# Pooled attention, SoLU and SiLU on one core: other places in the step table of the first SiLU matmul, and one reload issued by ACT

## The chip, the core and the metric

The kernel runs on one core of one Trainium2 chip. A core has five engines that work side by side, each through its own instructions in order: PE (matmuls, into PSUM), DVE, ACT and POOL (element by element work), and SP, which here only starts DMA transfers. DMA transfers started from any queue run on the core's 16 DMA engines. The metric is the device time of one execution in microseconds (us). Before the change it is 1367.52 us, the median of three runs (1366.87 to 1371.12).

## The reference

Three blocks follow each other, all in float32, on 8 x 576 = 4608 tokens:

```
k_p, v_p = k, v averaged over groups of 8 positions
attn = softmax(q @ k_p.T / 8) @ v_p                  # 8 heads of 64 -> x: 4608 x 512
h = x @ w_in (512 x 1024); solu = h * softmax(h)
x = layer_norm(solu) * g_ln @ w_out (1024 x 512)
h = x @ w_in2 (512 x 2048); g = h / (1 + exp(-h))    # SiLU
out = g @ w_out2 (2048 x 512)
```

The change lies in `h = x @ w_in2` and its SiLU, "the first SiLU matmul" below.

## The kernel before

Every operand is kept as a pair of rounded parts, high and low, and a product is three matmuls (high*high, high*low, low*high). The high part is made by ACT (a copy that rounds), the low part by DVE (a subtraction, line 529). Both SiLU matmuls use seven products of sums of quarters instead of eight products of quarters, so sums and differences of the quarters of both operands have to be made too.

The first SiLU matmul runs from about 609 to 1000 us of the profiled span. It is 12 passes, n = 0 to 11. A pass takes 768 tokens (one of six groups) and half of the 2048 columns of the weights; passes 0 to 5 use the first half, that is the weight sets 0 and 1, passes 6 to 11 the second half, sets 2 and 3. A pass has four steps (i = 0 to 3) of seven products, 28 products in all, of six matmuls each (line 709). Each product fills one of eight PSUM banks, which are taken in turn, and has one reader: the first and the third of a step are copied to SBUF by ACT (lines 724 and 729), the others are read by DVE additions (line 719). POOL adds two more sums per step into the result tile `gt`. ACT then takes SiLU of `gt` in two halves (line 677), and SP writes `gt` to DRAM as `gd` (line 679). There are two `gt` tiles, so step i must find the write of step i - 2 landed.

Beside the products other work is laid on the engines by a table of places. `plan(n, work, first)` puts each piece `(at, f)` at place `first + at * (28 - first) // 28` of pass n; place p is issued behind the reader of product p. On ACT, DVE, POOL and SP the order of the instructions is exactly the order in which the program writes them, so these numbers set the order of each engine's queue, and an instruction that has to wait holds up all that stands behind it on its engine. The pieces that matter here:

- `load_tokens(n)` (line 625, on SP): 768 tokens of the next pass, `x2r`, 1536 KB. There is one such buffer, so the load waits until the tokens before have been read for the last time.
- `tokens(n)` (lines 627 to 658): sums of token quarters on POOL (from pass 1 on), high parts on ACT (line 640), low parts on DVE, for the next pass. The first high part, of `r11`, and the first sum are its first pieces.
- `load_quad(q)` (line 540, on SP): the raw quarters of a weight set, `w2r`, two transfers.
- `quad_sums(q)` (lines 585 to 605), in passes 1 and 2: the sums S1 to S4 of weight sets 2 and 3, split (ACT line 592, DVE line 529) and written to DRAM as `wsd` (line 596), since the buffers for sets 2 and 3 are still in use. `load_sums(q)` (line 611) brings them back, four transfers of 512 KB: set 2 in pass 5 behind place 15, set 3 in pass 6 behind place 0. `quad_rest` makes the other three of each set at that time, from `w2r`.
- `load_rows(f)` (line 748, on SP): raw rows of the last weights, `wr`, in two buffers which `quad_sums` uses for its results before; `w2o_block(f)` (lines 752 to 784), from pass 3 on, splits them and writes them to DRAM as `wod` (line 775).

Each DMA gets one of eight landing semaphores, and a DMA that gets a semaphore again first waits for the one before on it to land.

Of the kernel before, what the change touches and what calls it, by code (L numbers as in the profile page):

```python
# [9 lines left out]
F32 = mybir.dt.float32  # L10
# [34 lines left out]
L11, L12, S4, L22, S1, S2, S3 = range(7)  # L45
# [37 lines left out]
def pooled_attention__solu__silu_kernel(  # L83
# [13 lines left out]
    nc = tc.nc  # L97
# [437 lines left out]
    wq, w2r = {}, {}  # L535

    def load_quad(q):
        w2r[q] = [pools["wr"].tile([P, 2, 512], F32, tag=f"w2r{h}", name="w2r") for h in range(2)]
        for h in range(2):
            nc.sync.dma_start(w2r[q][h], w2if[q][:, 2 * h : 2 * h + 2])  # L540
# [44 lines left out]
    def quad_sums(q):  # L585

        sum_, _, _, src = quarter(q)
        out = {}

        def hi(k, j):  # L590
            out[k] = pools["wx"].tile([P, 2, 512], F32R, tag=f"a{k % 2}", name="wo")
            nc.scalar.activation(out[k][:, 0], src[j], AF.Copy)

        def lo(k, j):
            sub(nc.vector, out[k][:, 1], src[j], out[k][:, 0].bitcast(F32))
            nc.sync.dma_start(wsd[q][k], out[k].bitcast(F32))

        work = [(2, lambda: sum_(S1)), (4, lambda: sum_(S2)), (12, lambda: sum_(S3))]
        for k, j in enumerate((S2, S1, S3)):
            work += [(7 + 4 * k, lambda k=k, j=j: hi(k, j)), (9 + 4 * k, lambda k=k, j=j: lo(k, j))]  # L600

        def fourth():
            sub(nc.vector, src[L12], src[L12], src[S2])

        return work + [(16, fourth), (19, lambda: hi(3, L12)), (21, lambda: lo(3, L12))]

    def load_sums(q):
        pool = pools["wq1" if q % 2 else "wq0"]
        for k, j in enumerate((S2, S1, S3, S4)):
            wq[q, j] = pool.tile([P, 2, 512], F32R, tag=f"w{j}", name=f"w2s{j}")  # L610
            nc.sync.dma_start(wq[q, j].bitcast(F32), wsd[q][k])

    def quad_rest(q, at):

# [8 lines left out]
    def load_tokens(n):  # L623
        x2r[n] = pools["x2r"].tile([P, KC, G2], F32, tag="x2r", name="x2r")
        nc.sync.dma_start(x2r[n], x2d[n % NG2])
# [58 lines left out]
    def plan(n, work, first=0, last=28):  # L684
        for at, f in work:
            slots.setdefault((n, min(first + at * (last - first) // 28, last - 1)), []).append(f)
# [59 lines left out]
    def load_rows(f):  # L746
        wrow[f] = pools["wx"].tile([P, 2, 2, 256], F32, tag=f"a{f % 2}", name="wr")
        nc.sync.dma_start(wrow[f].rearrange("p h d n -> p h (d n)"), w2of[f])
# [164 lines left out]
    for b in range(1, B):  # L913
        j = b // 2
# [149 lines left out]
    for n in range(N2):  # L1064
        if n == 0:
            plan(n, [(7 + at, f) for at, f in quad(1)])
            plan(n, tokens(1), 7)
            plan(n, [(14, lambda: load_quad(2)), (24, lambda: load_tokens(2))])
        elif n + 1 < N2:
            plan(n, tokens(n + 1))  # L1070
            if n + 2 < N2:
                plan(n, [(17, lambda n=n: load_tokens(n + 2))])
        if n in (1, 2):
            plan(n, quad_sums(n + 1))
            plan(n, [(23, lambda n=n: load_quad(3 if n == 1 else 2))])
        if n == 2:
            plan(n, [(23, lambda: load_rows(0))])
        if 3 <= n < N2 - 1:
            f = next(wout)
            plan(n, w2o_block(f))  # L1080
            if f + 1 < FC2 // 2:
                plan(n, [(3, lambda f=f: load_rows(f + 1))])
        if n == NG2 - 1:
            plan(n, quad_rest(2, 15) + [(15, lambda: load_sums(2)), (26, lambda: load_quad(3))])
        if n == NG2:
            plan(n, quad_rest(3, 3) + [(0, lambda: load_sums(3))])
        if n == N2 - 1:
            early = [pools["te"].tile([P, 3, 2, 256], F32R, tag=f"t{j}", name="w2o") for j in range(7)]
            home = ("raw", "raw", "raw", "w", "w", "w", "sign")
            more = [  # L1090
                stage.tile([P, 1, 2, 256], F32R, tag=home[j], name="w2o", bufs=1 if j == 6 else 3)
                for j in range(7)
            ]
            work = [(0, lambda: load_g(0)), (10, lambda: load_g(1))]
            for j in range(7):
                work += [(3 * j + 1, lambda j=j: load_part(0, j, early[j], nc.scalar)),
                         (21 + j, lambda j=j: load_part(1, j, more[j], nc.scalar))]
            s0 = lambda k: pools["wr"].tile([P, 512], F32, tag=f"w2r{k - 1}", name="s")
            lows = {}

            def high(m):
                lows[m] = prepare(m)

            work += [(10, lambda: sums_g(0, s0))]
            for m in range(7):
                work += [(14 + 2 * m, lambda m=m: high(m)), (15 + 2 * m, lambda m=m: lows[m]())]
            plan(n, work)
        for i in range(NPAIR):
            if (n, i) != (0, 0):
                hidden2(n, i)  # L1110
# [73 lines left out]
```

## Time and profile before

| what | value |
|---|---|
| median of three runs | 1367.52 us |
| the profiled execution | 1373.82 us, of which the profiled span is 1372.0 us |
| PE busy | 1282.5 us, 93% of the span |
| DVE, ACT, POOL busy | 73%, 52%, 48% |
| mean granted TensorE clock | 0.987 of full speed |

A matmul's record lasts longer than the distance to the next one, since matmuls are pipelined; PE's busy time is the time in which any record is open. A time in brackets behind a row is how long the engine had been idle, and the arrow names what ended the wait.

### The profile page before, as it was taken

Reading aid. Unit: us, or ns where it says so; the run is one execution under the profiler, and the core shown is the slowest. Engines: PE = TensorE matmul, PEld = TensorE weight load, DVE = VectorE, ACT = ScalarE, POOL = GpSimd, SP = SyncE. Lnnn points to the kernel's source line nnn. Section 1 sums busy time; section 2 is a strip of 40 time slices with the busy share of each in tenths; the row PEclk is TensorE's granted clock in tenths of the full one; section 3 lists DMA queues with packets and bytes.
Section 4 is the critical chain, followed back from the end, with each engine's and each line's share of the span. In section 5 each row is a group of like instructions: output and inputs, shape, how many; then the busy total and the mean of one; then the engine's idle time right before and its main releaser. Section 6 shows DMA issues by size and latency. Waiting matters only on the chain.

```text
span 1372.0 us, 23850 instructions
## 1 busy us (share of the span) xinstructions
PE 1282.5 (93%) x8712; PEld 1224.2 (89%) x8712; DVE 995.7 (73%) x1445; ACT 711.0 (52%) x1772; POOL 652.9 (48%) x822
## 2 busy tenths in 40 slices
PE   2579899999999999999999998999999999999998
PEld 2469788989898989899889998999999999999998
DVE  6996567766756654645877978899667888877785
ACT  4685555655655555534555655565434444444342
POOL 5675344444544433433666766687433343343332
PEclk9999999999999999999999999999999999999999
DMA  7655244444433411222467878666896334443431
GB/s 232 201 158 181 76 140 145 133 145 132 123 105 101 124 61 66 82 77 76 163 250 284 285 272 297 232 237 222 315 362 230 96 125 148 154 154 123 154 94 62
DMA packets 100549, 227.00 MB, mean 165 GB/s; under 512 B 8272, under 2 KB 29776, under 8 KB 98896
## 3 DMA queue, kind: packets, MB, share of 16 engines
q1 hardware_dynamic: 96400, 210.80, 46.4%
q10 hardware_dynamic: 4032, 14.68, 2.8%
q8 instruction: 69, 1.13, 0.3%
q14 instruction: 48, 0.39, 0.1%
HBM read 141.56 MB, written 83.89 MB: 164 GB/s over the span
## 4 chain that ended last, share of the span: by engine, by line
PE 52%; DMA 6%; DVE 5%; issue 3%; ACT 1%; POOL 1%; ACTq 0%; SPq 0%; DVEq 0%; POOLq 0%
PE op L857 24%; PE m L709 15%; PE xp L510 6%; PE hp L440 5%; DMA gd<-gt 2%; DMA wod<-wo 2%; DMA x2r<-x2d 1%; DMA w2r<-w2if 1%; DVE gt L719 1%; PE tp L490 1%; DVE t L529 1%; PE sp L311 1%; PE av L415 1%; POOL gt L719 0%; DMA w2o<-wod 0%
## 5 line engine op out<-in xcount | busy, mean ns | idle before, releaser
L709 PE MATMUL m<-t,w2s 128*128 128x384 f32 x2016 | 359.0, 338 | 16.8 <-DVE gt L719 7.4
L709 PEld LDWEIGHTS m<-t,w2s 128*128 128x128 f32 x2016 | 352.6, 190 | 22.8 <-DVE gt L719 8.8
L857 PE MATMUL op<-w2o,gt 128*128 128x256 f32 x3024 | 364.1, 283 | 2.6 <-ACT gt L834 2.2
L857 PEld LDWEIGHTS op<-w2o,gt 128*128 128x128 f32 x3024 | 363.2, 192 | 3.4 <-ACT gt L834 2.6
L529 DVE TENSOR_TENSOR gt<-gr,gt 128x512 fp32r<-128x512 f32 x180 | 166.9, 961 | 62.8 <-ACT gt L834 62.8
L834 ACT ACTIVATE gt<-gr 128x512 fp32r<-128x512 f32 x180 | 103.2, 623 | 150.7 <-DVE gr L529 127.9
L719 POOL TENSOR_TENSOR gt<-u,m 128x384 f32<-128x384 f32 x96 | 120.1, 1261 | 103.9 <-ACT m L729 48.0
L510 PE MATMUL xp<-lnh,w1oh 128*128 128x256 f32 x576 | 168.1, 292 | 0.6 <-ACT lnh L123 0.2
L510 PE MATMUL xp<-lnl,w1oh 128*128 128x256 f32 x576 | 164.3, 285 | 1.2 <-DVE lnl L124 1.2
L510 PE MATMUL xp<-lnh,w1ol 128*128 128x256 f32 x576 | 164.3, 285 | 0.0
L440 PE MATMUL hp<-w1ih,xTh 128*128 128x512 f32 x288 | 118.2, 410 | 9.4 <-DVE e L459 8.4
L329 ACT ACTIVATE pr<-sp,st 128x72 f32<-128x72 f32 x288 | 88.1, 330 | 57.3 <-POOL st L321 57.1
L440 PE MATMUL hp<-w1il,xTh 128*128 128x512 f32 x288 | 115.0, 399 | 0.6 <-POOL w1il L156 0.6
L440 PE MATMUL hp<-w1ih,xTl 128*128 128x512 f32 x288 | 115.0, 399 | 0.4 <-DVE xTl L124 0.4
L510 PEld LDWEIGHTS xp<-lnl,w1oh 128*128 128x128 f32 x576 | 111.8, 194 | 1.5 <-DVE lnl L124 1.4
L510 PEld LDWEIGHTS xp<-lnh,w1oh 128*128 128x128 f32 x576 | 111.6, 194 | 1.7 <-DVE lnl L124 1.1
L815 POOL TENSOR_TENSOR s<-gr 128x512 f32<-128x512 f32 x36 | 57.4, 1595 | 115.5 <-DVE gt L529 65.2
L510 PEld LDWEIGHTS xp<-lnh,w1ol 128*128 128x128 f32 x576 | 111.7, 194 | 0.0
L677 ACT ACTIVATE gt<-gt 128x768 f32<-128x768 f32 x96 | 80.6, 840 | 24.4 <-DVE gt L719 24.4
L440 PEld LDWEIGHTS hp<-w1ih,xTh 128*128 128x128 f32 x288 | 55.7, 193 | 21.6 <-issue 8.2
L834 ACT ACTIVATE gt<-s 128x512 fp32r<-128x512 f32 x72 | 42.1, 622 | 56.2 <-POOL s L529 54.3
L529 POOL TENSOR_TENSOR s<-s,gr 128x512 f32<-128x512 f32 x36 | 52.2, 1450 | 35.8 <-DVE gr L529 28.3
(130 smaller groups left out, 2306.7 us busy)
## 6 DMA issues: line engine op xcount, KB each, us to landing
gd<-gt SPq DMA_DIRECT2D x48, 768.0 KB, 4.5
gr<-gd SPq DMA_DIRECT2D x48, 512.0 KB, 6.4
x2r<-x2d SPq DMA_DIRECT2D x12, 1536.0 KB, 8.8
wod<-wo SPq DMA_DIRECT2D x56, 256.0 KB, 3.8
gr<-gd SPq DMA_DIRECT2D x48, 256.0 KB, 5.6
q<-qT SPq DMA_DIRECT2D x36, 256.0 KB, 3.2
raw<-kT SPq DMA_DIRECT2D x32, 288.0 KB, 3.4
x2d<-xo SPq DMA_DIRECT2D x18, 512.0 KB, 3.4
```

Of the source, the lines that this page charges most:

```text
L311: nc.tensor.matmul(sp[done : done + n, p // 2, (p % 2) * 2 * SP : (p % 2 + 1) * 2 * SP], q[:, p, done : done + n], kbd[b % 2][:, p, :], st ...
L329: behind["ACT"] = nc.scalar.activation(pr[:, g, h], sv[:, g, h], AF.Exp, scale=SCALE, bias=st[:, 0, g, h : h + 1], accum_out=st[:, 1, g, h ...
L415: nc.tensor.matmul(av[:, :n], l, r, start=(k == 0), stop=(k == 3))
L440: nc.tensor.matmul(hp[:, f], l, r, start=(n == 1 and m == 0), stop=(n == KC and m == 2))
L510: nc.tensor.matmul(xp[:, :GW], l, r, start=(k == 0 and m == 0), stop=(k == FC1 - 1 and m == 2))
L529: eng.tensor_tensor(dst, a, b, op=ALU.subtract)
L677: nc.scalar.activation(gt[:, h], gt[:, h], AF.Silu)
L709: nc.tensor.matmul(to, wt[:, a, o : o + P], tk[:, b, k], start=(k == 0 and m == 0), stop=(k == 1 and m == 2),)
L719: eng.tensor_tensor(dst, a, b, op=ALU.add)
L815: nc.gpsimd.tensor_tensor(s1, a21, a22, op=ALU.add)
L834: nc.scalar.activation(ring[n][:, 0], src, AF.Copy)
L857: nc.tensor.matmul(op[:, 256 * h : 256 * h + 256], t[:, l, i, ts], w[:, r], start=(s == i == h == m == 0), stop=(s == NSET - 1 and i == h ...
```

## The change

The table of places gets other numbers, and one transfer gets another issuer. In `quad_sums` the first two sums stand later (places 5 and 7 instead of 2 and 4), and the splits of the four sums stand three places apart instead of four, ending at place 20 instead of 21. The pieces of `tokens` in passes 1 to 10 start at place 2 instead of 0. `load_tokens(2)` in pass 0 goes from place 24 to 20, `load_quad` in passes 1 and 2 from 23 to 21, `load_rows(0)` in pass 2 from 23 to 20, ahead of `load_quad`. The reload of the sums is issued by ACT instead of SP.

```
-        work = [(2, lambda: sum_(S1)), (4, lambda: sum_(S2)), (12, lambda: sum_(S3))]
+        work = [(5, lambda: sum_(S1)), (7, lambda: sum_(S2)), (13, lambda: sum_(S3))]
         for k, j in enumerate((S2, S1, S3)):
-            work += [(7 + 4 * k, lambda k=k, j=j: hi(k, j)), (9 + 4 * k, lambda k=k, j=j: lo(k, j))]
+            work += [(9 + 3 * k, lambda k=k, j=j: hi(k, j)), (11 + 3 * k, lambda k=k, j=j: lo(k, j))]
...
-        return work + [(16, fourth), (19, lambda: hi(3, L12)), (21, lambda: lo(3, L12))]
+        return work + [(16, fourth), (18, lambda: hi(3, L12)), (20, lambda: lo(3, L12))]
...
-            nc.sync.dma_start(wq[q, j].bitcast(F32), wsd[q][k])
+            nc.scalar.dma_start(wq[q, j].bitcast(F32), wsd[q][k])
...
-            plan(n, [(14, lambda: load_quad(2)), (24, lambda: load_tokens(2))])
+            plan(n, [(14, lambda: load_quad(2)), (20, lambda: load_tokens(2))])
...
-            plan(n, tokens(n + 1))
+            plan(n, tokens(n + 1), 2)
...
-            plan(n, [(23, lambda n=n: load_quad(3 if n == 1 else 2))])
+            plan(n, [(21, lambda n=n: load_quad(3 if n == 1 else 2))])
...
-            plan(n, [(23, lambda: load_rows(0))])
+            plan(n, [(20, lambda: load_rows(0))])
```

SP's queue at the end of pass 0 (`gd_85` are the results of token group 0, `x2r` the tokens for pass 2; minus is before, plus is the change):

```order
 L679 DMA gd_85<-gt 256x1x768
 L540 DMA w2r<-w2if_93 128x1024 x2
+L679 DMA gd_85<-gt 256x1x768
+L625 DMA x2r<-x2d_81 128x3072
 L679 DMA gd_85<-gt 256x1x768 x2
-L625 DMA x2r<-x2d_81 128x3072
-L679 DMA gd_85<-gt 256x1x768
 L679 DMA gd_86<-gt 256x1x768
```

The load of the tokens for pass 2 now stands ahead of one more write of results, that of the third step of pass 0.

SP's queue from place 17 of pass 2 into pass 3 (`wsd` are the third and the fourth sum of set 3, `wr` the raw rows of blocks 0 and 1, `gd_87` the results of pass 2):

```order
 L625 DMA x2r<-x2d_83 128x3072
 L596 DMA wsd<-wo 128x1024 x2
-L679 DMA gd_87<-gt 256x1x768
+L748 DMA wr<-w2of_95 128x1024
 L540 DMA w2r<-w2if_93 128x1024 x2
-L748 DMA wr<-w2of_95 128x1024
-L679 DMA gd_87<-gt 256x1x768
+L679 DMA gd_87<-gt 256x1x768 x2
 L748 DMA wr<-w2of_96 128x1024
```

The first raw rows and the raw quarters now stand ahead of the last two writes of results of pass 2, and the rows ahead of the quarters. (The rows' buffer is that of the third sum, so the load waits until that `wsd` write has landed.)

ACT's queue at the start of pass 6, before (`gt` is the last result tile of pass 5, the names after `waits` are semaphores, DMAHW0 to 7 the landing semaphores):

```order
L724 ACTIVATE m_8898<-m 128x384 [waits DVE_49,PE_49,Activation_49]
L677 ACTIVATE gt<-gt 128x768 [waits DMAHW6_49,DVE_49]
L640 ACTIVATE t_8931<-x2r 128x768 [waits DMAHW0_49]
L729 ACTIVATE m_8899<-m 128x384 [waits PE_49,Activation_49,Pool_49]
L677 ACTIVATE gt<-gt 128x768 [waits DVE_49]
```

and the same place in the change:

```order
L724 ACTIVATE m_8898<-m 128x384 [waits DVE_49,PE_49,Activation_49]
L677 ACTIVATE gt<-gt 128x768 [waits DMAHW6_49,DVE_49]
L611 DMA w2s_8913<-wsd 128x1024 [waits DMAHW3_49]
L611 DMA w2s_8915<-wsd 128x1024 [waits DMAHW4_49]
L611 DMA w2s_8917<-wsd 128x1024
L611 DMA w2s_8919<-wsd 128x1024 [waits DMAHW1_49]
L729 ACTIVATE m_8899<-m 128x384 [waits PE_49,Activation_49,Pool_49]
L677 ACTIVATE gt<-gt 128x768 [waits DVE_49]
L640 ACTIVATE t_8942<-x2r 128x768 [waits DMAHW0_49]
```

Four transfers now stand in ACT's queue ahead of the copy of the third product, and three of them wait for the landing of an earlier transfer; the first high part of the next tokens went behind that copy.

## Rows read from the trace of the kernel before

**Rows 1.** The page: the engines' busy time; one kind of load (KB, us to landing).

```profile
PE 1282.5 (93%) x8712; PEld 1224.2 (89%) x8712; DVE 995.7 (73%) x1445; ACT 711.0 (52%) x1772; POOL 652.9 (48%) x822
...
x2r<-x2d SPq DMA_DIRECT2D x12, 1536.0 KB, 8.8
```

**Rows 2.** Windows, passes 1, 2, 3, 4, 6: length, busy PE, PEld, DVE, ACT, POOL; clock.

```profile
657.95:692.03 34.08, 31.28 (x169) 30.64 (x169) 28.04 (x36) 17.94 (x30) 19.87 (x12) 0.95 0.54 194
692.03:724.55 32.52, 30.40 (x170) 28.91 (x170) 25.47 (x36) 17.30 (x28) 19.80 (x12) 1.00 0.66 242
724.55:756.49 31.94, 29.79 (x169) 29.01 (x169) 24.71 (x35) 17.17 (x30) 21.02 (x16) 1.00 0.75 278
756.49:785.61 29.12, 29.12 (x169) 29.12 (x169) 27.99 (x40) 18.11 (x33) 24.39 (x17) 1.00 0.78 271
...
814.73:854.65 39.92, 33.15 (x170) 31.33 (x170) 31.57 (x42) 21.59 (x39) 23.59 (x18) 0.91 0.87 326
```

**Rows 3.** Timeline (start, length, engine, line, [idle before]): PE resuming, passes 1, 2, 3, 6.

```profile
670.55 5.65 PE L709 MATMUL m<-t,w2s 128*128 128x384 f32 x22 [2.03 <-ACT m L729]
...
704.71 5.62 PE L709 MATMUL m<-t,w2s 128*128 128x384 f32 x27 [1.07 <-DVE u L719]
...
739.93 1.33 PE L709 MATMUL m<-t,w2s 128*128 128x384 f32 x6 [1.70 <-DVE gt L719]
...
823.62 13.83 PE L709 MATMUL m<-t,w2s 128*128 128x384 f32 x77 [1.97 <-DVE t L529]
...
841.67 0.59 PE L709 MATMUL m<-t,w2s 128*128 128x384 f32 x2 [1.68 <-DVE gt L719]
844.13 2.29 PE L709 MATMUL m<-t,w2s 128*128 128x384 f32 x6 [1.88 <-DVE w2s L529]
```

**Rows 4.** Windows, two stretches at half clock, one of full transfers (last: DMA share, GB/s).

```profile
672.00:675.40 3.40, 3.40 (x13) 3.40 (x12) 3.40 (x6) 2.03 (x5) 3.40 (x3) 0.50 0.60 231
842.60:849.50 6.90, 5.37 (x17) 5.37 (x18) 6.90 (x12) 4.08 (x8) 2.74 (x3) 0.51 0.68 238
806.00:840.00 34.00, 30.78 (x172) 29.25 (x170) 24.99 (x35) 16.16 (x30) 17.60 (x14) 1.00 0.97 353
```

**Rows 5.** Timeline, tokens of pass 2: last read of the old ones, load, wait.

```profile
653.42 2.65 DVE L529 TENSOR_TENSOR t<-x2r,t 128x768 fp32r<-128x768 f32 x1
...
659.91 0.60 SPq L625 DMA_DIRECT2D x2r<-x2d  x1
...
669.28 0.84 ACT L640 ACTIVATE t<-x2r 128x768 fp32r<-128x768 f32 x1 [7.01 <-DMA x2r<-x2d]
```

**Rows 6.** Timeline, raw quarters in pass 2.

```profile
692.70 0.52 SPq L679 DMA_DIRECT2D gd<-gt  x1
693.27 2.25 SPq L540 DMA_DIRECT2D w2r<-w2if  x2
...
703.50 0.69 DVE L554 TENSOR_TENSOR wt<-w2r 128x512 f32<-128x512 f32 x1 [7.05 <-DMA w2r<-w2if]
```

**Rows 7.** Timeline, raw rows in pass 3.

```profile
721.55 3.18 SPq L596 DMA_DIRECT2D wsd<-wo  x2
...
729.57 0.32 SPq L748 DMA_DIRECT2D wr<-w2of  x1
...
737.37 0.42 ACT L770 ACTIVATE wo<-wr 128x256 fp32r<-128x256 f32 x1 [7.17 <-DMA wr<-w2of]
```

**Rows 8.** Timeline, passes 5 and 6: the reloads and two waits.

```profile
804.08 2.94 SPq L611 DMA_DIRECT2D w2s<-wsd  x4
...
817.21 0.42 ACT L770 ACTIVATE wo<-wr 128x256 fp32r<-128x256 f32 x1 [6.51 <-DMA wod<-wo]
...
824.89 2.57 SPq L611 DMA_DIRECT2D w2s<-wsd  x4
827.56 0.52 SPq L679 DMA_DIRECT2D gd<-gt  x1
...
838.04 0.56 DVE L719 TENSOR_TENSOR gt<-m,m 128x384 f32<-128x384 f32 x1 [2.66 <-DMA gd<-gt]
```

## The prediction

> **What bounds the kernel now.** On the page, first: PE is busy 1282.5 us, 93% of the span, and no other engine more than 73% [rows 1]. PE sets the end, so a change is worth what it takes out of PE's stops, and the question is where PE stops. Second, the windows, one per pass of the first SiLU matmul: six of the twelve run in 29.12 us with PE busy all of it (pass 4 stands for them), while passes 1, 2, 3 and 6 take 34.08, 32.52, 31.94 and 39.92 [rows 2]. Their excess is 4.96 + 3.40 + 2.82 + 10.80 = 21.98 us, and that is all that this change can win, since its places lie in these passes; pass 0 also loses time, but ahead of the place where its queue changes. Third, PE's own timeline, for what ended each stop: ACT's copy of a product in pass 1, a DVE addition in passes 2 and 3, DVE's low parts and additions in pass 6 [rows 3]. Fourth, the same passes on ACT, DVE and SP, for what those engines had been waiting for. There the answer is always a DMA: the tokens [rows 5], the raw quarters [rows 6], the raw rows [rows 7], a write that lies behind the reloaded sums and a result tile that is not yet written out [rows 8]. The stops of PE are thus late echoes: with eight banks and 29.12 / 28 = 1.04 us a product, a reader may be some seven products, 7.3 us, late before PE stands. The waits that did reach PE were of 6.5 to 7.2 us, on a reader already a few products behind.
>
> A stop costs more than its length. After those of pass 1 the granted clock stood at 0.50, the 1.2 GHz level, for 3.40 us, and after those of pass 6 at 0.51 for 6.90 us [rows 4]; PE, which had idled 2.03 us before the first and three times before the second [rows 3], lost 1.70 and about 3.4 us by that. With the stops this goes too.
>
> **The change part by part.**
>
> Pass 1, tokens for pass 2. DVE's last read of the old tokens ends at 653.42 + 2.65 = 656.07, but SP issues the load at 659.91, because a write of results stands ahead of it in SP's queue [rows 5]. The change puts the load ahead of that write: 3.84 us sooner. ACT's first high part also goes behind the copy of the third product. The wait of 7.01 us becomes at most 7.01 - 3.84 = 3.17, less what ACT does first, and what PE waited for, that copy, no longer stands behind it. So the stop of 2.03 and the half clock of 1.70 go. The other 1.23 us of the pass are short stops while DVE caught up; I take half. Gain 4.3, between 0 and 4.96.
>
> Pass 2, raw quarters of set 3. DVE stood 7.05 us at the sum S1, with the additions of the products behind it [rows 6]. Three things now bring load and use apart: S1 stands three places (3.1 us) later; the load goes ahead of a write of 768 KB, which at the 353 GB/s of a full stretch [rows 4] is 2.2 us, and 0.57 us for SP's issue (693.27 - 692.70) [rows 6]; and the last split that SP waits for is a place earlier. That is some 7 us, without counting that pass 1 no longer runs late. The stop of 1.07 goes, and the later ones by DVE's lateness mostly. Gain 2.8, between 0 and 3.40.
>
> The closer splits have a price: between the write of a sum and the reuse of its buffer lie four places now, 4.2 us, instead of six. ACT then may wait at a split for a `wsd` write to land: at most the 8.0 us that SP, in the last stretch of pass 2, took from such a write to the load that waits for it (729.57 - 721.55) [rows 7], at least nothing, and I take 2 us in each of the passes 1 and 2, since most of those 8.0 belong to the tokens ahead in the queue. ACT is busy 17.94 of 34.08 us [rows 2], so it makes that up, and PE sees none of it unless it comes on top of another wait.
>
> Pass 3, raw rows. ACT (and POOL) stood 7.17 us for them [rows 7]. In the change their load is asked for ahead of the raw quarters, but it must wait until the third `wsd` write has landed: before, that took the 8.0 us just named. SP stands meanwhile, and two writes of results stand behind it that were free to go. What decides is how late DVE makes the third split: 721.55 is 29 us into a pass [rows 2], for a piece of place 17. With the 7.05 us wait gone it comes at about 21, the write lands at about 29, and the rows about 3 us into pass 3, where they are asked for. The held results follow 1.5 MB of rows and quarters, 4.5 us at 353 GB/s, and land some 8 us into pass 3, while POOL wants their tile at 4 and DVE at 5: a new wait of 3 to 5 us, which is under the 7.3 us that the banks cover. Gain 2.0, between -7 (below, the slower rival) and 2.82.
>
> Passes 5 and 6, the reload. SP issued the first four transfers from 804.08 to 807.02, the second four from 824.89 to 827.46, and the write of the last results of pass 5 only behind these, at 827.56 [rows 8]. ACT stood 6.51 us for a small `wod` write that had been queued behind the first four, DVE 2.66 us for that write of results [rows 8]. From ACT the first four start about where they did, since its place is reached then; the second four start at about 817, just into pass 6, 8 us sooner. SP's writes stand behind neither. Four transfers of 512 KB are 2.1 MB, or 5.9 us at 353 GB/s [rows 4]: the `wod` lands sooner by half of that, if both queues share the DMA engines, and by all of it at best, 3 to 6 us, which takes the stop of 1.97. The results go out 2.7 us sooner (827.56 - 824.89) and share in the same, about 5 us, which takes most of the other stops. Against it: in pass 6 ACT's queue now waits for the landing of earlier transfers ahead of the copy of the third product. The nearest rows are the four issues of 2.94 us and the wait of 6.51 us [rows 8]; from below it is nothing, where those have landed. I take 3 us, and the banks cover it. DVE itself is busy 31.57 us in this pass [rows 2], so unless its instructions shorten the pass stays at 31.6 and no more than 8.35 is to be had. Gain 6.4, between 0 and 8.4.
>
> The Trainium skill bears on this edit from two sides. "DMA: Bandwidth & Descriptors", Queues, rings and completion order, says that each DMA engine takes packets in turn from the queues that have work, so that SP's small writes would pass the 2 MB from ACT's queue; the trace of before has no two such queues side by side here. The same page, Issuing engines are not separate DMA queues, says that starting transfers from another engine only saves the time of issuing; by that sentence alone pass 6 would win no more than the 2.57 us of issues [rows 8]. What would follow from it is the first rival.
>
> Passes 4, 5 and 7 to 11: only the first pieces of the tokens move, by one or two places. No pass there has a stop to lose, and their ACT and POOL then meet the tokens' landing later: 0.
>
> **Sum.** 4.3 + 2.8 + 2.0 + 6.4 = 15.5 us off the profiled execution's 1373.82 (its span of 1372.0 and 1.8 around it), 1358.3. That execution is 6.3 us over the median of 1367.52. If all of those 6.3 were stops of this kind, a usual execution has only 15.7 us of excess and wins 15.5 x 15.7 / 21.98 = 11.1; if none, 15.5. I take 14 for the median: 1353.5.
>
> **Rivals.**
> - *The transfers are the bound from pass 5 on.* From 806 to 840 the DMA engines are 97% busy [rows 4], so another queue shuffles the same bytes, and ACT waits where SP did. For it: that number. Against it: what was late were single small writes behind 2 MB, and transfers can start sooner. Pass 6 then wins nothing and pass 3 half: 4.3 + 2.8 + 1.0 = 8.1, for the median about 7.3: 1360.2.
> - *DVE is the bound of passes 1, 2 and 6.* It is busy 28.04 us in pass 1, against 29.12 for PE, and 31.57 in pass 6 [rows 2], so its lateness stays and the stops come back at other products. Against it: in pass 4 it is busy 27.99 and PE has no stop [rows 2]. If passes 1 and 2 take 32 each and the rest hardly moves, the gain is 2.1 + 0.5 + about 0.5: 1364.5.
> - *Slower: SP is held by the raw rows.* One mechanism, at the end of pass 2. If DVE makes the third split as late as before, the rows are asked for at 729.5, the quarters after them, and the results that had gone out before the end of the pass start at about 731; at the 8.8 us that a load of twice the size takes to land [rows 1] POOL and DVE stand until about 740, 14 us from the start of pass 3's use of the tile. Less the 7.3 us of the banks that is a stop of near 7 and a half clock like the 3.4 of pass 6: 10 instead of 2.8. If passes 1 and 2 then win 2 and pass 6 nothing, it is 5 us slower: 1372.5. It decides where that split comes later than about 25 us into pass 2.
>
> **How the numbers follow.** The forecast has 0.60, with a range of its own of 1347 to 1358; the transfers as bound 0.19; DVE as bound 0.12; slower 0.06; and 0.03 that nearly all 21.98 us go, 1345.5. Within 0.3%, 4.1 us, a measurement of this kernel can't be told from no change. Faster than that are the forecast, the first rival and the last case, 0.82; no change is the second rival, 0.12; slower 0.06. The range is 1346 to 1363: it takes in the forecast, the first rival and most of the bounds of pass 6, and leaves out the other two rivals and the extreme.
>
> **What would show it.** Right: passes 1, 2 and 3 at 29.1 to 30 us; ACT no longer stands for the tokens in pass 1, nor DVE for `w2r` in pass 2, nor ACT for `wr` in pass 3; pass 6 at 32 to 35 us with one stop or none; no half clock at either place. Step by step wrong: pass 6 still near 39 with the waits on `gd` and `wod` unchanged, or a long wait in front of ACT's four issues (first rival); DVE without idle time through passes 1 and 2 and PE waiting for its additions (second); POOL and DVE waiting 8 us or more for `gd` at the start of pass 3 (third). The forecast as a whole is wrong if passes 4, 5 or 7 to 11 show stops that they don't have now.

## The result: slower by 0.8%, and the profile after

The changed kernel takes 1380.11 us (median of 4 executions, 1378.49 to 1383.35), the kernel before beside it 1368.43 us (4 executions): a ratio of 1.0081, interval 1.0065 to 1.0097. That is 11.7 us slower, where 14 us faster was forecast. The profiled execution took 1380.22 us, its span is 1378.1.

Windows of the changed kernel: passes 1, 2, 3, 4, 6 and 11, and two stretches at half clock (columns as in [rows 2]).

```profile
656.31:685.97 29.66, 29.44 (x169) 29.05 (x169) 28.08 (x35) 17.25 (x29) 20.40 (x12) 1.00 0.56 206
685.97:720.71 34.74, 31.13 (x170) 28.81 (x170) 27.62 (x36) 17.07 (x28) 20.15 (x12) 1.00 0.61 228
720.71:759.80 39.09, 32.00 (x170) 30.85 (x169) 27.52 (x37) 18.16 (x32) 21.79 (x16) 0.91 0.68 235
759.80:789.86 30.06, 29.41 (x170) 29.09 (x169) 27.04 (x36) 17.37 (x31) 21.46 (x16) 1.00 0.67 236
819.85:857.33 37.48, 31.98 (x169) 30.65 (x169) 32.17 (x44) 21.82 (x39) 24.05 (x18) 0.91 0.87 325
974.31:1005.81 31.50, 29.64 (x171) 29.21 (x171) 14.62 (x27) 10.96 (x20) 11.13 (x10) 1.00 0.96 357
741.41:745.09 3.68, 3.68 (x11) 3.68 (x12) 3.16 (x4) 3.65 (x8) 3.68 (x4) 0.50 0.19 71
847.51:850.87 3.36, 3.36 (x10) 3.36 (x11) 3.36 (x6) 0.11 (x1) 1.99 (x2) 0.50 0.63 242
```

Against [rows 2], pass 1 won 4.42 us, as forecast (4.3), and pass 6 won 2.44. But pass 2 lost 2.2, pass 3 lost 7.15, and passes 4, 5, 10 and 11, which had stood at 29.1 to 29.3, lost 0.94, 0.87, 0.50 and 2.22. PE's timeline says who ended the stops; these are the first stop of pass 2, the two long ones of pass 3, the one of pass 4 and the long one of pass 6, and they answer to [rows 3]:

```profile
699.00 1.32 PE L709 MATMUL m<-t,w2s 128*128 128x384 f32 x6 [0.38 <-DVE gt L719]
...
737.68 1.50 PE L709 MATMUL m<-t,w2s 128*128 128x384 f32 x6 [4.33 <-DVE gt L719]
741.41 10.46 PE L709 MATMUL m<-t,w2s 128*128 128x384 f32 x48 [2.23 <-DVE gt L719]
...
782.46 29.41 PE L709 MATMUL m<-t,w2s 128*128 128x384 f32 x168 [0.66 <-DVE gt L719]
...
847.51 12.76 PE L709 MATMUL m<-t,w2s 128*128 128x384 f32 x62 [4.72 <-DVE w2s L529]
```

Pass 2 has seven stops of 0.36 to 0.92 us, all by DVE's additions: each time PE waited for DVE to free a bank, so at each of them DVE was late by all eight banks. What DVE, POOL and ACT had waited for stands in the timeline of passes 2 to 4 (SP, DVE, POOL and ACT; SP's rows hold a start and the time taken by the issue or issues grouped there):

```profile
686.50 2.77 SPq L540 DMA_DIRECT2D w2r<-w2if  x2
689.37 2.11 SPq L679 DMA_DIRECT2D gd<-gt  x2
...
698.38 0.56 DVE L719 TENSOR_TENSOR gt<-m,m 128x384 f32<-128x384 f32 x1 [6.98 <-DMA gd<-gt]
...
698.45 1.00 POOL L719 TENSOR_TENSOR gt<-u,m 128x384 f32<-128x384 f32 x1 [9.16 <-DMA gd<-gt]
699.40 2.55 POOL L529 TENSOR_TENSOR tt<-x2r 128x768 f32<-128x768 f32 x1
...
701.98 0.84 ACT L640 ACTIVATE t<-tt 128x768 fp32r<-128x768 f32 x1 [9.98 <-POOL tt L529]
...
718.02 3.19 SPq L596 DMA_DIRECT2D wsd<-wo  x2
726.21 0.32 SPq L748 DMA_DIRECT2D wr<-w2of  x1
726.58 0.90 SPq L540 DMA_DIRECT2D w2r<-w2if  x2
727.60 1.48 SPq L679 DMA_DIRECT2D gd<-gt  x2
...
737.06 0.56 DVE L719 TENSOR_TENSOR gt<-m,m 128x384 f32<-128x384 f32 x1 [10.92 <-DMA gd<-gt]
...
767.11 1.02 POOL L719 TENSOR_TENSOR gt<-u,m 128x384 f32<-128x384 f32 x1 [4.72 <-DMA gd<-gt]
768.08 2.55 POOL L529 TENSOR_TENSOR tt<-x2r 128x768 f32<-128x768 f32 x1
```

The first lines of pass 6 in the same view, beside [rows 8]: ACT's issues, and the two waits, which went from 6.51 to 3.42 and from 2.66 to 1.35 us.

```profile
821.90 0.42 ACT L770 ACTIVATE wo<-wr 128x256 fp32r<-128x256 f32 x1 [3.42 <-DMA wod<-wo]
825.82 2.49 ACTq L611 DMA_DIRECT2D w2s<-wsd  x4
...
840.23 0.56 DVE L719 TENSOR_TENSOR gt<-m,m 128x384 f32<-128x384 f32 x1 [1.35 <-DMA gd<-gt]
```

Two things are to be seen in passes 2 to 4. First, SP: the results of the third step of pass 1 go out only behind the raw quarters, at 689.37, 3.4 us into pass 2 instead of 0.67 (692.70 in [rows 6], pass from 692.03). At the end of pass 2, SP stands from 721.21 (718.02 + 3.19) to 726.21 until the third `wsd` write has landed, with the results of pass 2's third step behind it: DVE waits 10.92 us for the tile, until 16.35 us into pass 3. The wait for `w2r` of [rows 6] is gone; a wait for the result tile took its place. Second, POOL: its first token sum (`tt`) now stands behind the addition that waits for that tile. It starts 13.4 us into pass 2 and 8.3 us into pass 4, and in pass 2 ACT, with copies of products queued behind, waits 9.98 us for it.

### The profile page after: what moved, and what is told of

The parts are those of the page before. It is cut to its first block, busy times and chain, and to the rows that moved or that the text cites. A ratio compares the mean times of both kernels' runs of the same rounds, so it can differ in the third digit from the quotient of the medians.

```text
span 1378.1 us, 23832 instructions
## 1 busy us (share of the span) xinstructions
PE 1286.6 (93%) x8712; PEld 1226.5 (89%) x8712; DVE 1005.7 (73%) x1445; ACT 712.1 (52%) x1772; POOL 656.9 (48%) x822
## 4 chain that ended last, share of the span: by engine, by line
PE 55%; DVE 6%; DMA 4%; issue 2%; ACT 1%; POOL 1%; SPq 0%; ACTq 0%; DVEq 0%; POOLq 0%
PE op L857 25%; PE m L709 17%; PE xp L510 6%; PE hp L440 5%; DMA gd<-gt 3%; DVE gt L719 1%; DVE t L529 1%; PE tp L490 1%; DVE wo L529 1%; PE sp L311 1%; DMA wsd<-wo 1%; DVE w2r L529 1%; PE av L415 1%; DMA w2o<-wod 0%; DVE u L719 0%
## 5 line engine op out<-in xcount | busy, mean ns | idle before, releaser
L719 POOL TENSOR_TENSOR gt<-u,m 128x384 f32<-128x384 f32 x96 | 124.1, 1299 | 135.7 <-DMA gd<-gt 62.0
```

Of the source, the lines that this page charges most:

```text
L719: eng.tensor_tensor(dst, a, b, op=ALU.add)
```

## The experiments

Ratios are to the kernel before, run beside each kernel, with 95% intervals; differences between kernels are differences of these ratios, times 1368 us. Passes are lengths in the one profile of each kernel (us; 29.1 is no stop, pass 11 29.3); the last column sums all twelve. before_again is a single execution.

| kernel | median us | ratio | 1 | 2 | 3 | 4 | 6 | 11 | sum |
|---|---|---|---|---|---|---|---|---|---|
| before | 1368.43 | 1 | 34.1 | 32.5 | 31.9 | 29.1 | 39.9 | 29.3 | 390.9 |
| before_again | 1372.74, one | | 33.9 | 32.2 | 31.9 | 29.1 | 37.0 | 29.3 | 387.5 |
| changed | 1380.11 | 1.0081 (1.0065-1.0097) | 29.7 | 34.7 | 39.1 | 30.1 | 37.5 | 31.5 | 398.0 |
| quad23 | 1373.45 | 1.0020 (1.0006-1.0034) | 29.6 | 31.5 | 34.6 | 30.2 | 38.0 | 31.1 | 389.6 |
| rows23 | 1376.74 | 1.0048 (1.0031-1.0064) | 29.5 | 34.9 | 35.3 | 29.7 | 37.9 | 30.2 | 392.9 |
| both23 | 1374.25 | 1.0025 (1.0008-1.0042) | 29.3 | 31.4 | 36.0 | 29.7 | 37.0 | 30.9 | 389.1 |
| gd_act | 1375.01 | 1.0043 (1.0026-1.0060) | 30.8 | 33.8 | 32.9 | 31.6 | 37.5 | 29.3 | 397.0 |
| tok0 | 1364.93 | 0.9977 (0.9960-0.9994) | 29.1 | 32.3 | 37.5 | 29.1 | 35.2 | 29.3 | 386.6 |
| pool0 | 1369.90 | 0.9994 (0.9977-1.0010) | 29.2 | 33.0 | 37.8 | 29.1 | 35.3 | 29.3 | 387.7 |
| split0 | 1377.07 | 1.0044 (1.0025-1.0064) | 29.6 | 34.9 | 40.1 | 29.1 | 38.4 | 29.3 | 395.4 |
| b_first2 | 1379.87 | 1.0068 (1.0044-1.0091) | 33.2 | 33.6 | 36.1 | 29.1 | 41.8 | 31.6 | 399.7 |
| b_tok20 | 1364.57 | 0.9960 (0.9945-0.9975) | 29.1 | 32.0 | 31.9 | 29.1 | 38.4 | 29.3 | 383.8 |
| b_actreload | 1367.44 | 0.9979 (0.9963-0.9995) | 34.5 | 32.4 | 31.8 | 29.1 | 34.1 | 29.3 | 385.1 |
| two_parts | 1359.13 | 0.9919 (0.9895-0.9943) | 29.1 | 31.4 | 31.9 | 29.1 | 33.2 | 29.3 | 378.2 |
| tok0_both23 | 1362.89 | 0.9942 (0.9918-0.9965) | 29.1 | 29.2 | 36.2 | 29.1 | 33.8 | 29.3 | 380.8 |
| two_w2o6 | 1363.11 | 0.9950 (0.9932-0.9968) | 29.1 | 31.0 | 29.1 | 34.6 | 33.8 | 29.3 | 381.0 |
| two_w2o3 | 1361.44 | 0.9928 (0.9899-0.9956) | 29.1 | 31.8 | 30.4 | 29.1 | 35.9 | 29.3 | 379.8 |
| sums_w2o3 | 1358.32 | 0.9904 (0.9880-0.9928) | 29.1 | 29.6 | 33.3 | 29.1 | 35.1 | 29.3 | 379.5 |

### First theory: SP's order

**quad23**, the changed kernel with

```
-            plan(n, [(21, lambda n=n: load_quad(3 if n == 1 else 2))])
+            plan(n, [(23, lambda n=n: load_quad(3 if n == 1 else 2))])
```

> The changed kernel with load_quad of passes 1 and 2 back at place 23, behind the write of the results of step 2; all else as changed. Theory A (SP's order): in the changed kernel these results wait in SP's queue behind the raw quarters, go out 3.4 us into pass 2 and land at 12.3 us, and DVE stands 6.98 us and POOL 9.16 us for the tile. With the quarters behind them again DVE's wait falls under 3 us, pass 2 goes from 34.7 to 30-32 us, and the third split of pass 2 comes 3 us earlier. Pass 3 keeps the held rows, which still stand ahead of the results: 34-37 us instead of 39.1. In all 5 to 9 us faster than the changed kernel, about 1372. Theory B (DVE's work stands too close in the new places): both passes stay within 1 us of 34.7 and 39.1, the time within 2 us of 1380.

Pass 2 31.5, pass 3 34.6, 8.3 us faster than the changed kernel: as theory A expected, but for DVE's wait in pass 2, which stayed at 3.65 us.

**rows23**: `load_rows(0)` from place 20 back to 23. **both23**: both edits.

> The changed kernel with load_rows(0) of pass 2 back at place 23, behind the quarters and the results of step 2; all else as changed. Theory A: SP stood 5.0 us (721.2 to 726.2) for the third wsd write, with the results of step 2 behind it, which landed 16.3 us into pass 3. These results now go out before SP stands: they land 5 us sooner, DVE's wait of 10.9 us in pass 3 becomes about 6, the stops of 4.33 and 2.23 us and the half clock behind them go mostly, pass 3 takes 31-34 us instead of 39.1; pass 2 is as in the changed kernel, 34.7. In all 5 to 8 us faster than the changed kernel, about 1373. Theory B: no change within 2 us.

> The changed kernel with load_quad and load_rows(0) both back at place 23, so that SP's order in passes 1 to 3 is that of before; the closer sums, the tokens from place 2, the earlier tokens for pass 2 and ACT's reload stay. Theory A: the waits for the result tile at the start of passes 2 and 3 fall to 3 us or less, passes 2 and 3 take 30-32 us each, and the time is 10 to 14 us under the changed kernel, 1366-1370 or better, at or under the kernel before. Theory B: passes 2 and 3 stay DVE bound, 33 us or more each; the time stays over 1373.

rows23 won 4.5 us, most of it in pass 3 (35.3, where 31 to 34 was expected). both23 failed the theory: SP's order is that of before, pass 2 takes 31.4, but pass 3 still 36.0, and the 7.7 us won are no more than with the quarters alone. So a part of the loss was not SP's order.

**gd_act** takes the results off SP altogether:

```
-                nc.sync.dma_start(gd[g][:, f :: FC2 // 2], gt.rearrange("p a b n -> p a (b n)"))
+                nc.scalar.dma_start(gd[g][:, f :: FC2 // 2], gt.rearrange("p a b n -> p a (b n)"))
```

> The changed kernel with every write of results issued by ACT, behind its own SiLU, instead of SP; all else as changed, the quarters and rows at 21 and 20. Theory A: the results stand behind nothing in SP's queue any more, so DVE's waits for the tile in passes 2 and 3 (6.98 and 10.9 us) fall to 4 us or less, and passes 2 and 3 take 29.5-32 us; each issue costs ACT's queue some 0.5 us, four in a pass in which ACT is busy 18 of 29 us, so nothing is lost by it. The time is 10 to 16 us under the changed kernel, about 1366. Theory B: passes 2 and 3 stay over 33 us and the time over 1375. A third way: ACT's issues wait for landings ahead of copies that PE needs, and stops of PE behind ACT's copies come up all over passes 1 to 11; then it is slower than 1380.

A miss for theory A: 5.2 us, not 10 to 16. Pass 3 fell by 6.2 us, but pass 2 by 0.9 only, and passes 4, 5, 9 and 10 grew to 31.6, 30.7, 30.3 and 33.4. Its timeline around the start of pass 2, at 686.54:

```profile
681.26 0.56 ACTq L679 DMA_DIRECT2D gd<-gt  x1
681.41 0.32 SPq L625 DMA_DIRECT2D x2r<-x2d  x1
...
687.51 0.55 ACTq L679 DMA_DIRECT2D gd<-gt  x1
...
693.48 0.56 DVE L719 TENSOR_TENSOR gt<-m,m 128x384 f32<-128x384 f32 x1 [4.99 <-DMA gd<-gt]
...
697.42 1.02 POOL L719 TENSOR_TENSOR gt<-u,m 128x384 f32<-128x384 f32 x1 [1.91 <-DMA gd<-gt]
```

By the trace's landing times the first of the two writes, of pass 1's second step, landed 12.1 us after its issue, and that ended DVE's wait, in the last step of pass 1; the second landed after 9.7 us and ended POOL's. In the changed kernel SP issued the first of them at 680.69, ahead of the tokens' load, and it landed in 4.5 us. So the queue was not all: the write went out at once and still landed late, beside SP's transfers (the tokens' load, issued 0.15 us after it, took 9.0 us, and two sums and the raw quarters followed). In passes 3, 4, 8 and 9 the write behind the tokens' load landed 8.1 to 9.3 us after its issue, in the changed kernel 7.0 to 7.3; that fits the growth of the passes behind them, but no run tests it. What else made the changed kernel slow was the next question.

### The parts by themselves

**tok0**, the changed kernel with

```
-            plan(n, tokens(n + 1), 2)
+            plan(n, tokens(n + 1))
```

> The changed kernel with the tokens' pieces of passes 1 to 10 starting at place 0 again; all else as changed. Theory C: the start at place 2 is what gives passes 4, 5, 10 and 11 their new stops at product 20 (18 in pass 11), which take 0.94 + 0.87 + 0.50 + 2.22 us, since the late token pieces crowd into the second half of a pass on DVE. They go: these four passes take 29.1-29.4 us. Passes 2 and 3 keep their waits for the result tile, since SP's order is that of the changed kernel: 34-35 and 38-40 us. In all about 4.5 us faster than the changed kernel. Rival: these stops come from the later issue of the rows and the results (ACT's reload, SP's order), and stay; then no change within 1.5 us.

14.2 us come back, three times what theory C expected: passes 4, 5, 10 and 11 lose their stops as it said, and passes 2, 3 and 6 win 2.4, 1.6 and 2.3 on top. This kernel beats the one before, by 0.2%.

**b_tok20** and **b_actreload**, the kernel before with one part each:

```
-            plan(n, [(14, lambda: load_quad(2)), (24, lambda: load_tokens(2))])
+            plan(n, [(14, lambda: load_quad(2)), (20, lambda: load_tokens(2))])
```
```
-            nc.sync.dma_start(wq[q, j].bitcast(F32), wsd[q][k])
+            nc.scalar.dma_start(wq[q, j].bitcast(F32), wsd[q][k])
```

> The kernel before with load_tokens(2) of pass 0 at place 20 instead of 24, nothing else. Theory A: this part alone takes the stop and the half clock out of pass 1 (34.1 to 29.3-30 us) as the changed kernel shows, and costs nothing elsewhere, since the write of results that it passes is not waited for until the tile's next use. Passes 2 and 3 stay within 1 us of 32.5 and 31.9. 4 to 5 us faster than before in the profile, 3 to 5 in the median. Rival: the tokens of pass 3 and the raw quarters don't come sooner, so what pass 1 wins is waited for in pass 2, which goes to 35 us or more; no change within 1 us.

> The kernel before with the four reloads of passes 5 and 6 issued by ACT instead of SP, nothing else. Theory A: pass 6 takes 37-38 us instead of 39.9, as in the changed kernel; its long stop, before the low part of the last quarter at product 20, stays or grows to 4.7 us, since the raw quarters of set 3 still come late and DVE makes its pieces late. All other passes as before. 2 to 3 us faster. Rival: the gain of pass 6 in the changed kernel came from pass 5's or the tokens' other places; then pass 6 stays at 39 to 40 and the time within 1 us of before.

Both go the way of theory A, by -5.5 us (a little more than the 3 to 5 expected) and -2.9 us; in b_actreload pass 6 is 34.1, shorter than the 37 to 38 expected, and its last stop kept its 1.88 us. The timeline of b_actreload in pass 6 (from 814.21) shows why, beside [rows 8]:

```profile
814.47 0.42 ACT L770 ACTIVATE wo<-wr 128x256 fp32r<-128x256 f32 x1 [4.29 <-DMA wod<-wo]
...
818.39 2.25 ACTq L611 DMA_DIRECT2D w2s<-wsd  x4
...
825.20 0.52 SPq L679 DMA_DIRECT2D gd<-gt  x1
...
832.62 0.56 DVE L719 TENSOR_TENSOR gt<-m,m 128x384 f32<-128x384 f32 x1 [0.60 <-DMA gd<-gt]
```

ACT's wait for the `wod` write went from 6.51 to 4.29 us, the second reload starts 4.2 us into the pass instead of 10.2 (824.89 - 814.73), the results follow at 11.0 instead of 12.8, and DVE waits 0.60 us for them instead of 2.66. The Trainium skill ("DMA: Bandwidth & Descriptors", Issuing engines are not separate DMA queues) says that starting transfers from another engine saves only the issuing time. Here the four issues take about as long on ACT (2.25 us) as on SP (2.57 in [rows 8]). The time alone (-2.9 us, uncertain by some 2) does not tell more than those 2.57 us; the rows do: the reload and the results start sooner in the pass, and what stood behind the reloads is waited for less.

**before_again** is the kernel before, profiled once more.

> The kernel before, unchanged, profiled once more on this chip. If the excess of passes 1, 2, 3 and 6 (4.96, 3.40, 2.82 and 10.80 us) is the same in every execution, it stands here within 0.5 us each, and the 6 us by which the profiled execution lay above the median of before came from elsewhere. If it is not, one or more of them is 2 us or more smaller here, and the sum of the twelve passes (390.9) is nearer to 386.

Passes 1, 2 and 3 repeat within 0.3 us; pass 6 took 37.04 instead of 39.92, and 38.4 in b_tok20, whose edit lies six passes ahead of it. So my 10.80 us of excess was the highest of three samples.

### Tokens from place 2, and the good parts together

**b_first2**: the kernel before with `tokens(n + 1), 2` alone.

> The kernel before with the tokens' pieces of passes 1 to 10 starting at place 2 instead of 0, nothing else. Theory D: the first pieces of the tokens stand, at place 0, ahead of the additions that wait for the result tile, and run while those would wait; at place 2 they stand behind them, and POOL's chain of token sums and DVE's low parts of a pass start some 5 us later, so DVE runs at the banks' limit through the rest of the pass. Then this alone is 7 to 12 us slower than before, passes 4, 5, 10 and 11 have a stop at product 18 to 20 each (1 to 2 us in a pass), and pass 6 has a long stop at product 20. Rival: the places only hurt together with SP's new order and the closer sums; then the time is within 3 us of before and passes 4, 5, 10 and 11 keep 29.1 us.

9.3 us slower: the places hurt without SP's new order. Of the details, passes 4 and 5 stayed at 29.1, against theory D; passes 3, 6 and 11 carry most of the loss (36.1, 41.8, 31.6).

**two_parts** is b_tok20 and b_actreload in one. **tok0_both23** is that and the new places of `quad_sums`, as in the change.

> The changed kernel with tokens from place 0 and with the quarters and the rows back at place 23: of the change only the places of the sums, the earlier tokens for pass 2 and ACT's reload are left. Beside the next kernel it differs in the places of the sums alone. Theory A (the place of the sums helps, since S1 then finds its quarters): passes 2 and 3 take 30-31 us each, pass 3 losing what SP's order cost the kernel with tokens from 0 alone (37.5), and the time is 1357-1361. Rival: the closer splits bring nothing, since the third split is made as late as before by a DVE that is late in any case: passes 2 and 3 stay at 31.5-32.5, and the time is that of the next kernel within 1.5 us.

> The kernel before with only the two parts that won by themselves: load_tokens(2) at place 20 (-5.2 us) and the reloads issued by ACT (-2.4 us). The two act in passes that are four apart: if they add, pass 1 takes 29.1-29.3, pass 6 34 us or a little over, passes 2 and 3 32 each, and the time is 7 to 8 us under before, about 1362. Rival: one of the two waits only moves (pass 6 varies from 37.0 to 39.9 in the kernel before by itself), and the time is 1364 or more.

two_parts: 11.1 us under before, at least the sum of its parts. tok0_both23: pass 2 falls to 29.2, so the places of the sums do their work, but pass 3 rises to 36.2, against both views, and the time is 3 us over two_parts, within the intervals. First tok0_both23 (pass 3 from 713.85), then two_parts (from 714.59): third `wsd` write, issue of the raw rows, their first use.

```profile
710.90 3.19 SPq L596 DMA_DIRECT2D wsd<-wo  x2
...
720.24 0.32 SPq L748 DMA_DIRECT2D wr<-w2of  x1
...
729.08 0.42 ACT L770 ACTIVATE wo<-wr 128x256 fp32r<-128x256 f32 x1 [8.18 <-DMA wr<-w2of]
```
```profile
711.59 3.18 SPq L596 DMA_DIRECT2D wsd<-wo  x2
...
719.53 0.32 SPq L748 DMA_DIRECT2D wr<-w2of  x1
...
727.38 0.42 ACT L770 ACTIVATE wo<-wr 128x256 fp32r<-128x256 f32 x1 [7.21 <-DMA wr<-w2of]
```

Counted from the start of pass 2 (684.67 and 683.20) the third sum goes out after 26.2 and 28.4 us, yet the rows are there after 44.4 and 44.2 us: the same in both. Two landings in a row set it, that of the third sum and that of the rows, and in both kernels the sum's write landed 1.2 us after the 1.5 MB of tokens ahead of it in SP's queue: 9.2 us after its issue in the one, 7.8 in the other. The closer sums shortened pass 2 by 2.2 us and so brought the use of the rows nearer, not the rows: they come 15.2 instead of 12.8 us into pass 3, and the stop there is 4.09 us instead of 1.68, with a half clock behind it.

**two_w2o6** lets the use wait instead: two_parts with `plan(n, w2o_block(f), 6 if n == 3 else 0)`.

> The kernel of the two parts with the splits of the first raw rows in pass 3 starting at place 6 instead of 0. Before, ACT stood 7.17 us in pass 3 for rows that were loaded too late, with copies of products behind it. If work behind a late load belongs behind the work that doesn't need it, this wait shrinks to 1 us or less, the stop of 1.7 us at product 12 goes, and pass 3 takes 29.1-30.5 instead of 31.9: 1 to 3 us faster than the two parts alone. Rival: the splits, crowded into the rest of the pass, make DVE late as the tokens from place 2 do; pass 3 gets stops at products 18 to 25 and is no shorter.

Pass 3 has no stop left, but pass 4 one of 3.38 us, and the kernel is 4.2 us slower than two_parts (uncertain by some 4), where 1 to 3 us faster was expected. From the end of pass 3 into pass 4 (from 749.82):

```profile
746.43 0.57 SPq L625 DMA_DIRECT2D x2r<-x2d  x1
747.20 2.45 SPq L775 DMA_DIRECT2D wod<-wo  x2
...
756.31 0.42 ACT L770 ACTIVATE wo<-wr 128x256 fp32r<-128x256 f32 x1 [5.95 <-DMA wod<-wo]
```

Two small writes now stand behind the 1.5 MB of the tokens, where one did, and ACT waits 5.95 us for a buffer: the same trap, one pass on.

### Which piece of the tokens

**pool0** and **split0** are the changed kernel with, in place of `plan(n, tokens(n + 1), 2)`,

```
work = tokens(n + 1)
plan(n, work[:4])          # split0: plan(n, work[:4], 2)
plan(n, work[4:], 2)       # split0: plan(n, work[4:])
```

The first four pieces are POOL's sums. In pool0 the orders of DVE, ACT and SP are those of the changed kernel; POOL's differs by this (plus is pool0):

```
+L529 TENSOR_TENSOR tt<-x2r 128x768
 L719 TENSOR_TENSOR gt<-u_7245,m_7244 128x384
-L529 TENSOR_TENSOR tt<-x2r 128x768
```

> The changed kernel with POOL's four token sums of a pass planned from place 0 again; the high and low parts stay from place 2, so that the order of ACT, DVE and SP is that of the changed kernel and only POOL's differs: its first token sum stands ahead of the result addition that waits for the result tile, not behind it. Theory D1 (POOL's chain): POOL, which stood 4.7 us in pass 4 for the tile with the first sum behind, does the sum meanwhile; passes 4, 5, 10 and 11 go back to 29.1-29.5, and 7 us or more of the 14 come back: 1366-1373. Rival D2 (ACT's and DVE's parts): the order of DVE decides; these passes keep 29.6-31.5 and the time stays within 3 us of the changed kernel's 1380.

> The changed kernel with the high and low parts (ACT and DVE) of the tokens planned from place 0 again and POOL's token sums from place 2. Theory D1: POOL's first sum still stands behind the waiting result addition, and ACT's part of it (of T1) now waits for POOL earlier in ACT's queue; little comes back, less than 4 us: 1376 or more. Rival D2: DVE's and ACT's places decide; passes 4, 5, 10 and 11 take 29.1-29.4 and 7 us or more come back.

pool0 wins 11.9 us, split0 5.1 (each uncertain by some 3; together more than the 14.2 of tok0, so the two overlap). So the order on POOL, of the compute engines the one that is busy least, makes up most of the 14 us; DVE's and ACT's places have a share, and for passes 4, 5, 10 and 11 either of the two is enough, against D1. POOL in passes 2 to 4 of pool0 (from 688.87, 721.91 and 759.71):

```profile
693.38 1.85 POOL L529 TENSOR_TENSOR tt<-x2r 128x768 f32<-128x768 f32 x1 [1.21 <-DMA x2r<-x2d]
700.77 2.69 POOL L719 TENSOR_TENSOR gt<-u,m 128x384 f32<-128x384 f32 x2 [5.55 <-DMA gd<-gt]
...
726.39 1.86 POOL L529 TENSOR_TENSOR tt<-x2r 128x768 f32<-128x768 f32 x1 [1.15 <-DMA x2r<-x2d]
...
764.23 1.85 POOL L529 TENSOR_TENSOR tt<-x2r 128x768 f32<-128x768 f32 x1 [2.62 <-DMA x2r<-x2d]
```

The first sum starts 4.5 us into each pass (the changed kernel: 13.4, 17.4 and 8.3; the kernel before 4.7, 3.8 and 4.9), as soon as its tokens have landed, and is done before the wait for the tile. Behind it hang ACT's split of it (701.98 in the changed kernel, after 9.98 us of standing), three more sums and DVE's low parts.

**two_w2o3** and **sums_w2o3** are two_parts and tok0_both23 with the splits of the rows in pass 3 from place 3 and the tokens' load of that pass at 18.

> The kernel of the two parts with the splits of the first raw rows in pass 3 starting at place 3 instead of 0, and the tokens' load of pass 3 at place 18 instead of 17, so that no more small writes stand behind it than in the two parts. Expected: the wait of 7.2 us for the rows shrinks by about 3, the stop of 1.7 us in pass 3 goes, pass 3 takes 29.1-30.5 and pass 4 stays at 29.1-30: 1357-1359, at or just under the two parts. Rival: as with the start at place 6, the last splits come late and pass 4 waits for their writes behind the tokens: pass 4 takes 31 us or more and the time is over the two parts.

> The same two edits on the kernel with the closer sums, tokens from 0 and SP's order of before. If pass 3 there lost 4.3 us (36.2 to 31.9) only because its use of the raw rows came sooner after the third split, by the 2.2 us that pass 2 had won, then a start 3 places later gives most of it back: pass 2 stays at 29.2, pass 3 takes 29.5-32.5, and the time is 1355-1359. Rival: the splits are late for DVE's sake and pass 3 stays over 34.

Passes 3 and 4 as expected in two_w2o3 (30.4, 29.1), though its median of 1361.44 is no better than two_parts. sums_w2o3 has 1358.32 us, 0.9904, the best ratio of all, but pass 3 at 33.3 is longer than expected, and its interval overlaps that of two_parts for the most part. Which of the two is faster stays open; both are some 1% under the kernel before and 1.6 to 1.8% under the changed one.

## Why the prediction was wrong

Taking the edits in turn by their ratios: the two good parts -11.1 us; the places of the sums +3 (within the intervals); quarters and rows sooner +4.8 (tok0 less tok0_both23); tokens from place 2 +14.2. Together +11.1. The shares hold for this order alone: the tokens from place 2 cost 9.3 us by themselves (b_first2), and 11.4 with SP's order as it was (both23 less tok0_both23).

- **The step that failed most** is "Passes 4, 5 and 7 to 11: only the first pieces of the tokens move, by one or two places. No pass there has a stop to lose". It priced the move at nothing because PE had no stop there, without naming what stood in the engine's queue between the old place and the new one. On POOL that was the addition that waits for the result tile, and the move cost every pass that had late results, passes 2, 3 and 6 too. What had covered the sum, and the prediction named nowhere, was that wait itself: the sum used to run inside it. What the runs showed in place of the 0 is 9.3 us (b_first2) to 14.2 (tok0), and 11.9 for POOL's order alone (pool0).
- **Pass 2.** "the load goes ahead of a write of 768 KB" was counted as 2.2 us won for the quarters. It was not asked who waits for that write: DVE and POOL, 6.98 and 9.16 us. Forecast a gain of 2.8, measured a loss of 2.2. The mechanism for the wait for `w2r` was right, as pass 2 of tok0_both23 shows (29.2).
- **Pass 3.** "With the 7.05 us wait gone it comes at about 21" failed: the third split came 32.05 us into pass 2 (718.02 - 685.97), and in tok0_both23, with no such wait, still at 26.2 (710.90 - 684.67). A place is not a time: readers run up to eight products late, so place 17 lies at 18 us plus up to eight. What followed is the slower rival's wait: it put the end of POOL's and DVE's wait at 740, which was 15.5 us into that pass, and the pass's excess at 10 instead of 2.8; they waited until 16.35 us, and the excess is 39.09 - 29.12 = 9.97. I had given it 0.06. That the excess fits so closely is in part luck: 1.6 us of it come from the tokens' places (tok0), and with those and SP's order as before pass 3 still takes 36.2 (tok0_both23), since ACT and POOL then wait 8.2 us for the raw rows. Behind the wait for the tile stood another.
- **Pass 1** was right: 4.3 forecast, 4.96 in b_tok20, which also shows that the tokens alone were the cause.
- **Pass 6** was right in mechanism: b_actreload takes out 5.9 us beside the profile of before, 3.0 beside before_again, and 2.9 by its ratio, where 6.4 was said. The term was sized from one execution, in which this pass was at its longest. ACT's issues did not wait; the 3 us set aside for that were 0 (four issues in 2.49 us). In the changed kernel the tokens took 2.3 us of the gain back (35.2 in tok0), by a stop of 4.72 us instead of 1.89.
- **The rivals.** The transfers as the bound did not hold: pass 6 fell to 33.2 in two_parts at the same bytes. DVE as the bound described pass 2 of the changed kernel, but as a consequence of late starts: with the tokens from 0 and SP's order as before the same work fits in 29.2 (tok0_both23).

Not settled: the share of DVE's order in the loss by the tokens, what is left of pass 3, and why pass 6 varies.

## What to carry to other kernels

Before an instruction is moved, list what stands between the old place and the new one on its engine's queue, and for each of these who waits for it or what it waits for; a move past a waiting instruction costs that wait, on the idlest engine too. Where two DMA landings in a row set when the data is there, a shorter pass before its use does not make it come sooner: in tok0_both23 it lengthened the wait from 7.2 to 8.2 us. A part that wins by itself is found by running it by itself: here two of the parts were worth 11 us and the others lost 22 together.

## What the runs showed of the hardware

- A pass may differ by 2.9 us between two executions of the same program (pass 6: 39.92 in [rows 2], 37.04 below), and the first SiLU matmul began anywhere from 604.4 to 612.1 us in the 18 profiles, though no kernel here changes anything ahead of it. A single profile's span can't judge such changes; medians can, and pass lengths where they differ by more than that. Whether the two executions ran on the same chip is not on record.

```profile
816.29:853.33 37.04, 32.42 (x170) 31.16 (x170) 31.99 (x42) 21.61 (x39) 24.02 (x18) 0.91 0.86 315
```

- Stops that together came to 6.56 us in pass 3 of the changed kernel were followed by 3.68 us at a granted clock of 0.50, the 1.2 GHz level; the seven stops of under 1 us each in pass 2 were not (clock 1.00 over the pass). The length of a stop alone does not tell: one of 2.03 us in pass 1 before was followed by 3.40 us at 0.50 ([rows 3], [rows 4]), one of 2.38 us in pass 2 of tok0 by none (clock 1.00 over the pass).
- A write of 768 KB that landed 4.5 us after its issue from SP, ahead of a 1.5 MB load in the same queue, landed after 12.1 us when ACT issued it 0.15 us before SP issued that load (the changed kernel and gd_act); the load took 9.8 and 9.0 us. There, being issued first did not make the smaller transfer land first.
